# Batch 0 turned in whole blocks, output weights prepared while it is pooled, and a planner that weighs TensorE's work by array area

## The chip, the cores and the metric

One core of a Trainium2 chip runs the kernel. The metric is the device time in microseconds of one launch, from inputs in HBM to the output in HBM. The engines are TensorE (PE; its weight loads are listed as PEld), VectorE (DVE), ScalarE (ACT) and GpSimd (POOL); SyncE (SP) issues nearly all transfers. Each engine runs its instructions in the order in which the program lists them.

## The reference

Four batches of 12608 rows of 128 floats go through two attentions with 32 inducing points, and then each row goes through a feed-forward block with 1024 hidden values.

```python
def mab(q, kv):                         # per batch
    s = scale * (q @ kv.T); a = exp(s - s.max(-1)); a /= a.sum(-1) + 1e-9
    return a @ kv
h   = mab(inducing, x)                  # 32 x 128: x is pooled over all rows
y   = mab(x, h)                         # 12608 x 128
hid = y @ w_in                          # 12608 x 1024
e   = exp(hid - hid.max(-1)); solu = hid * e / (e.sum(-1) + 1e-9)
ln  = (solu - mean(solu)) / sqrt(var(solu) + 1e-6) * g_ln
out = ln @ w_out                        # 12608 x 128
```

The weights come as 64-bit floats.

## The kernel before

**Tiling.** A batch is 99 slots of 128 rows (the last is half full). Three stages work on it. `p1(b, k)` pools x in nine groups of up to 12 slots. `p2(b, j)` computes the second attention's normalised exponentials for up to 12 slots. `main()` then takes each slot as a *tile*: four matmuls give the 1024 hidden values in PSUM (L1058), VectorE scales them and takes the minimum (L1093), ScalarE exponentiates (L1103), GpSimd multiplies (L1108), ScalarE squares and sums (L1123), VectorE transposes in 32x32 blocks (L1136), and for each four tiles `products` accumulates 128 matmuls with the output weights `wc` on TensorE (L1183). There are 396 tiles. While a batch's tiles run, the next batch is pooled between them; batch 0 has nothing to hide behind.

**Pooling of batch 0.** `p1(0, k)` loads a group (L429), turns each slot on TensorE, and ScalarE copies the turned group to SBUF (L676). Turning is done by `turned_rows` (L595): four transposes of 32 rows for each slot, in two halves `w`, one for each pair of row quarters. Then come scores (L722), a running maximum through VectorE and a small matmul (L741 to L774), exponentials on ScalarE (L785), a VectorE transpose (L805), the pooling matmuls (L815) and the sum `acc` (L829, L831). The turned x goes to a DRAM buffer (L695) and is read again by `p2` (L909). Loads go to a list of buffers, EARLY_X, that borrows memory free at that time: two pieces of `wc`, seven of `spare` and two of its own. The exponentials borrow pieces of `wc` and of the output staging `os`.

**Weights.** `rounded` (L471) turns 64-bit floats to 32-bit ones in integer steps on VectorE (L483 to L492, L501), one on ScalarE (L494) and products and sums on GpSimd (L497 to L504). `weights_in` does it for w_in, `weights_out` for w_out, through the same five scratch buffers `conv`, so each step of the second waits for one of the first. `weights_out` then multiplies by the gains (L526), takes the mean over 1024 with matmuls (L535), subtracts it (L540), waits until all of batch 0 is pooled, because `wc` is lent, and spreads the rows over `wc` with 16 transfers (L556). The mean's PSUM tile comes from H, which is filled by `handover`.

**Handover.** `handover()` waits for the last pooled group, for the hidden weights of batch 0 (`hw_ready`, last copy L883) and for the first two `p2` groups' reads; then it closes the early PSUM pool and gives its banks and the borrowed SBUF to the tiles.

**The order.** Nothing is scheduled at run time. A planner runs while the program is built: each task yields operations with a cost in nanoseconds and a priority, and `Planner.run` picks for each engine, among the operations that would be ready, the one with the smallest priority. Constants at the head of the file (PR_..., P1_..., WOUT, WIN, LATE, FILL) shift these priorities. `_pe` models TensorE's clock from the busy share of stretches, and where TensorE would be idle for more than FILL ns, `_fill` puts in filler transposes of the identity (L564). The program begins with 32 such transposes (`warm`, L573).

Of the kernel before, what the change touches and what calls it, by code (L numbers as in the profile page):

```python
# [57 lines left out]
HEAD = 1  # L58
HEAD_PR = 2.3
# [9 lines left out]
P2_AHEAD = 47.6  # L69
P2_START = 24  # L70
PR_EX = -5.12
PR_EV = -13.85
PR_FI = -34.53
PR_G2 = 16.08
PR_HN = -4.97
ENDING = 16
PR_MD = 23.27
PR_MU = -7.99
PR_SQ = 2.19
PR_SA = 9.01  # L80
PR_SP = -11.4
PR_ED = -4.49
PR_EA = -8.32
PR_TU = 1.01
RUSH = 8.71
TURN_NS = 62
# [3 lines left out]
WARM = 32  # L90
WOUT = -14.2
WIN = -25.77

# [10 lines left out]
DMA_RATE = 360.0  # L104
WINDOW = 4096 / 1.2


def kind(eng):
    return "PE" if eng[:2] == "PE" else eng


class Done:


    def __init__(self, eng, end):
        self.eng, self.end = eng, end


class Op:
    def __init__(self, eng, cost, fn, *after, prio=None, alt=None, moves=0, tail=0, turn=False):  # L120
# [23 lines left out]
class Planner:  # L144


    def __init__(self, slack):
        self.clock = dict(BEGIN)
        self.ops, self.blocked, self.seq, self.slack = [], 0, 0, slack
        self.window, self.busy, self.slow, self.until = 0, {}, True, 0.0  # L150
# [61 lines left out]

    def _pe(self, start, cost):

        at = start
        while True:
            k = int(at // WINDOW)
            while self.window < k:
                busy = self.busy.get(self.window, 0.0) / WINDOW
                self.slow = busy < 0.8 if self.slow else busy < 0.7  # L220
                self.window += 1
            room = max(1.0, (k + 1) * WINDOW - at)
            rate = 2.0 if self.slow else 1.0
            took = min(room, cost * rate)
            self.busy[k] = self.busy.get(k, 0.0) + max(0.0, at + took - max(at, self.until))
            at += took
            self.until = max(self.until, at)
            cost -= took / rate
            if cost < 1.0:
                return at - start  # L230
# [38 lines left out]
    def run(self):  # L269
        clock = self.clock  # L270
        while self.ops:
# [22 lines left out]
            op.fn()  # L294
            end = start + (self._pe(start, cost) if kind(eng) == "PE" else cost)
            for e in PARTS.get(eng, (eng,)):
# [10 lines left out]
def set_attention_then_solu_kernel(ctx: ExitStack, tc: tile.TileContext, x, inducing, w_in, w_out, g_ln, out):  # L307
# [32 lines left out]
    def buf(shape, name, dtype=F32, where=None):  # L340
        return (where or const).tile(shape, dtype, name=name)
# [33 lines left out]
    S2 = Lock([(buf([P, AG, M], f"s2_{i}"), buf([P, AG], f"mx{i}"), buf([P, AG], f"nr{i}")) for i in range(2)])  # L375
    A4 = Lock([buf([P, AG * 2 * M], "a4")])
    AT = Lock([(buf([P, AG // 2, P], f"aT{i}"), buf([P, AG], f"rn{i}")) for i in range(2)])
# [90 lines left out]
    hw_ready, wc_ready, ind_ready = [Event() for _ in range(NB)], Event(), Event()  # L468
    w_in_ready = Event()

# [45 lines left out]
    def weights_out():  # L516
        wg2 = hn_b[2]
        wg = wg2.rearrange("p (k d) -> p k d", k=KC)
        g = yield from rounded(wg2, w_out.bitcast(U32).rearrange("(k p) d -> p k d", p=P), conv, conv_free, conv_end, WOUT)
        for i in range(EUS):  # L520
            give(EU, eu_b[:, i, :], g)
        give(HN, hn_b[1], g)
        gd = yield dma(4096, lambda: nc.sync.dma_start(g_sb, g_ln.rearrange("(k p) -> p k", p=P)))

        def gain(k):
            return lambda: nc.scalar.activation(wg[:, k, :], wg[:, k, :], AF.Copy, scale=g_sb[:, k : k + 1])  # L526

        for k in range(KC):
            d = yield Op("ACT", 251, gain(k), g, gd, prio=LATE)
# [7 lines left out]
        d = yield Op("PE", KC * 215, mean, g, rel, prio=LATE)  # L537
        d = yield Op(
# [3 lines left out]
            ),  # L542
            d, prio=LATE,
        )
        give(H, mp, d)
        for k in range(NP):
            yield p1_done[0][k]
        o = yield Op("POOL", 200, lambda: nc.gpsimd.memset(wc[:, :, C : C + 1], 1.0), [d for e in p1_done[0] for d in e.after])
        o_end = [o]
        rows = wc.rearrange("p (k q) d -> p k q d", q=4)  # L550
        spread = []
        for a in range(4):
            for q in range(4):
                c = yield dma(
                    M * FF * 4,
                    lambda: nc.sync.dma_start(rows[a * M : (a + 1) * M, :, q, :C], wg[q * M : (q + 1) * M]), d, o, issue=600, prio=LATE,  # L556
                )
                spread.append(c)
# [9 lines left out]
    def points():  # L568
# [5 lines left out]

        yield Op("PE", 107 * WARM, warm)
        d = yield dma(M * C * 4, lambda: nc.sync.dma_start(ind_sb, inducing))
# [61 lines left out]
    each = PG * C  # L638
    wc_flat = wc.rearrange("p j d -> p (j d)")
    EARLY_X = Lock([f[:, i * each : (i + 1) * each].rearrange("p (s c) -> p s c", c=C) for f, n in ((wc_flat, 2), (spare, SPARES * FF // each)) for i in range(n)] + xn_b)  # L640
    EARLY_T = Lock([vt_all[:, i * each : (i + 1) * each].rearrange("p (s t) -> p s t", t=P) for i in range(3 * GS * FF // each)] + [xT_b])
    e2 = [wc_flat[:, 2 * each : 2 * each + PG * M], wc_flat[:, 2 * each + PG * M : 2 * each + 2 * PG * M]] + [o.rearrange("p s c -> p (s c)")[:, : PG * M] for o in os_b[:2]]
    EARLY_EW = Lock([(e2[i], e2[i + 1].rearrange("p (s m) -> p s m", m=M)) for i in (0, 2)] + [ew_b])
# [6 lines left out]
    def p1(b, k):  # L650
# [23 lines left out]
        def copy(w, tr, d):  # L674
            def go():
                nc.scalar.copy(in_rows(xT[:, :n, :], w), from_rows(tr, n))  # L676

            d = yield Op("ACT", 94 + 48 * n, go, d, rel, tuple(ready), prio=None if early else RUSH)
# [5 lines left out]
        for w in range(2):  # L684
            tr, trel = yield ltr
            d = yield from turned_rows(tr, [(xn[:, s, :], P) for s in range(n)], w, None if early else RUSH, *[d for d, _ in xd], *trel)
            spawn(copy(w, tr, d), PRIO_P1(b, k))
        if early:
# [58 lines left out]
        if early:  # L747
# [6 lines left out]
            )  # L754
            d = yield Op("PE", 250, lambda: nc.tensor.matmul(mq, lhsT=fold2, rhs=v["mdiag"], start=True, stop=True), d, rel)
        else:
# [636 lines left out]
    for k in range(NP):  # L1393
        spawn(p1(0, k), PRIO_P1(0, k))
    spawn(weights_in(), -16)
    spawn(weights_out(), WOUT)
    spawn(handover(), 0)
# [30 lines left out]
```

## Time and profile before

| | us |
|---|---|
| median of three runs | 1169.65 |
| lowest, highest | 1164.29, 1173.36 |
| span of the profiled execution | 1170.7 |

The profile is of a further execution and gives its span, from the first to the last instruction; no separate time stands beside it. In its rows an engine's busy time is a union of its instructions; "x" counts them. [...] The ends of matmuls are modelled, so neighbouring rows of TensorE overlap by some 0.07 us. A releaser in square brackets names what ended an engine's idle time.

### The profile page before, as it was taken

To read this page: it belongs to the slowest core of one execution; us is meant where nothing else is said; L and a number is where in the kernel's file an instruction comes from. 1 tells how busy PE (TensorE), PEld (TensorE's weight loads), DVE (VectorE), ACT (ScalarE), POOL (GpSimd) and SP (SyncE) were. 2 spreads that over 40 slices of the span, in tenths; PEclk is the share of its full clock that TensorE was granted. 3 is DMA by queue.
4 is the path that set the end of the run, shared out by engine and by line. 5 is a ranking of instruction groups with operands and counts; after the bars stand their busy time and mean duration, and the time that the engine had idled before them with its cause. 6 is when DMAs were issued, how large, how long until landed. Compare 5 with 4: busy or idle time off the path is not lost.

```text
span 1170.7 us, 69841 instructions
## 1 busy us (share of the span) xinstructions
PE 1148.1 (98%) x31176; PEld 1037.0 (89%) x31176; DVE 1095.0 (94%) x1732; ACT 1105.3 (94%) x2325; POOL 1042.8 (89%) x648
## 2 busy tenths in 40 slices
PE   9989999999999999999999999999999999999997
PEld 7658988989899988999899998898899999989997
DVE  4679999999999999999999999999999999999995
ACT  4579999999999999999999999999999999999995
POOL 2379899888989999899999999899999999999994
PEclk8679999999999999999999999999999999999999
DMA  9472254453245245353223445453132323121112
GB/s 354 174 140 77 66 155 107 108 156 85 58 95 151 63 119 168 93 164 65 79 43 118 114 115 136 115 138 105 36 92 38 98 38 93 38 83 25 26 42 64
DMA packets 203405, 117.99 MB, mean 101 GB/s; under 512 B 148160, under 2 KB 156256, under 8 KB 202976
## 3 DMA queue, kind: packets, MB, share of 16 engines
q1 hardware_dynamic: 202928, 113.46, 36.5%
q8 instruction: 244, 4.00, 1.5%
q14 instruction: 57, 0.47, 0.1%
q10 hardware_dynamic: 176, 0.07, 0.0%
HBM read 53.57 MB, written 51.50 MB: 90 GB/s over the span
## 4 chain that ended last, share of the span: by engine, by line
PE 62%; ACT 11%; POOL 10%; DVE 7%; issue 5%; DMA 3%; SPq 1%; POOLq 0%; ACTq 0%; DVEq 0%
PE op L1183 43%; PE h L1058 6%; POOL eu L1108 5%; ACT sq L1123 4%; ACT eu L1103 4%; DVE vt L1136 3%; PE h L595 3%; POOL xn L1108 2%; DVE spare L1093 2%; PE h L940 2%; PE h L722 2%; DVE hn L1093 1%; PE h L815 1%; PE bank_t L595 1%; POOL xT L1108 1%
## 5 line engine op out<-in xcount | busy, mean ns | idle before, releaser
L1183 PEld LDWEIGHTS op<-wc,vt 32*128 32x128 f32 x25600 | 937.2, 185 | 52.2 <-issue 35.4
L1183 PE MATMUL op<-wc,vt 32*128 32x129 f32 x25600 | 970.2, 273 | 3.4 <-issue 1.0
L1108 POOL TENSOR_TENSOR eu<-spare,eu 128x1024 f32<-128x1024 f32 x231 | 545.7, 2382 | 27.5 <-ACT eu L1103 27.4
L1136 DVE STREAM_TRANSPOSE vt<-eu 128x1024 f32<-128x1024 f32 x351 | 429.1, 1231 | 4.7 <-POOL eu L1108 4.4
L1058 PE MATMUL h<-hs,aT 32*128 32x512 f32 x1584 | 409.0, 609 | 2.3 <-ACT xT L676 0.8
L1123 ACT ACTIVATE sq<-eu 128x1024 fp8e4<-128x1024 f32 x351 | 367.4, 1050 | 3.0 <-POOL eu L1108 3.0
L1093 DVE TENSOR_SCALAR_CACHE_REDUCE spare<-h,rn 128x1024 f32<-128x1024 f32 x247 | 309.1, 1255 | 9.9 <-PE h L1058 7.2
L1108 POOL TENSOR_TENSOR eu<-hn,eu 128x1024 f32<-128x1024 f32 x118 | 279.5, 2378 | 21.7 <-ACT eu L1103 21.3
L1103 ACT ACTIVATE eu<-spare,nm 128x1024 f32<-128x1024 f32 x232 | 265.2, 1144 | 0.9 <-DVE vt L1136 0.3
L1093 DVE TENSOR_SCALAR_CACHE_REDUCE hn<-h,rn 128x1024 f32<-128x1024 f32 x149 | 186.6, 1256 | 6.5 <-PE h L1058 4.5
L1058 PEld LDWEIGHTS h<-hs,aT 32*128 32x128 f32 x1584 | 123.1, 187 | 18.5 <-issue 6.3
L1103 ACT ACTIVATE eu<-hn,nm 128x1024 f32<-128x1024 f32 x119 | 136.1, 1144 | 1.4 <-DVE hn L1093 0.8
L1108 POOL TENSOR_TENSOR xn<-hn,xn 128x1024 f32<-128x1024 f32 x30 | 71.0, 2381 | 0.1
L1123 ACT ACTIVATION_READ_ACCUMULATOR sq<-eu 128x1 f32 x351 | 68.0, 194 | 0.0
L1282 ACT ACTIVATE os<-spare,fin 128x128 f32<-128x128 f32 (+1 forms) x200 | 62.0, 390 | 3.2 <-DMA out_dram<-os 1.8
L595 PE MATMUL h<-ident,xn 32*128 32x32 f32 x1188 | 46.4, 220 | 3.1 <-DMA xn<-in_x_dram 2.7
L595 PEld LDWEIGHTS h<-ident,xn 32*128 32x128 f32 x1188 | 45.0, 137 | 4.7 <-DMA xn<-in_x_dram 3.1
L1103 ACT ACTIVATION_READ_ACCUMULATOR eu<-spare,nm 128x1 f32 x232 | 44.9, 193 | 0.0
L676 ACT COPY xT<-h 128x768 f32<-128x768 f32 (+2 forms) x54 | 39.5, 733 | 1.8 <-PE h L1058 0.7
L1209 DVE COPY spare<-op 128x387 f32<-128x387 f32 (+1 forms) x75 | 36.0, 508 | 4.8 <-PE op L1183 4.3
L987 ACT COPY aT<-h 128x384 f32<-128x384 f32 (+3 forms) x82 | 32.7, 408 | 8.1 <-PE h L595 8.1
L595 PEld LDWEIGHTS h<-ident,a 32*128 32x128 f32 (+1 forms) x800 | 34.6, 137 | 6.3 <-issue 2.4
(187 smaller groups left out, 963.7 us busy)
## 6 DMA issues: line engine op xcount, KB each, us to landing
xT<-xd SPq DMA_DIRECT2D x93, 256.0 KB, 3.6
out_dram<-os SPq DMA_DIRECT2D x78, 256.0 KB, 3.2
xd<-xT SPq DMA_DIRECT2D x73, 256.0 KB, 3.2
xn<-in_x_dram SPq DMA_DIRECT2D x72, 256.0 KB, 3.5
dl<-dd SPq DMA_DIRECT2D x396, 1.0 KB, 2.6
a<-a SPq DMA_DIRECT2D x27, 192.0 KB, 4.3
xd<-vt SPq DMA_DIRECT2D x6, 768.0 KB, 7.2
spare<-in_x_dram SPq DMA_DIRECT2D x5, 768.0 KB, 10.9
```

The lines of the kernel that those rows point to most:

```text
L595: nc.tensor.transpose(out=tr[:h, at : at + M], in_=block[rows, :h], identity=ident[rows, rows])
L676: nc.scalar.copy(in_rows(xT[:, :n, :], w), from_rows(tr, n))
L987: lambda: nc.scalar.copy(in_rows(aT[:h, qa:qb, :], w), from_rows(tr, nq)[:h, qa:qb]),
L1058: nc.tensor.matmul(hp[:, cols], lhsT=aT[rows, i // 2, :], rhs=hs[rows, cols], start=True, stop=True)
L1093: lambda: nc.vector.tensor_scalar(out=hn, in0=hp, scalar1=rn, scalar2=None, op0=ALU.mult, op1=ALU.min, accum_out=nm),
L1103: "ACT", 1133, lambda: nc.scalar.activation(e, hn, AF.Exp, bias=nm, scale=-1.0, accum_out=G["qe"][:, s, 1:2]), d, rel, srel,
L1108: return lambda: eng.tensor_tensor(out=e, in0=hn, in1=e, op=ALU.mult)
L1123: nc.scalar.activation(sq_b[0], e, AF.Square, scale=1.0 / 32.0, saturate=False, accum_out=G["qe"][:, s, 0:1])
L1136: lambda: nc.vector.transpose(out=G["vtb"][:, : n * FF].rearrange("p (j s t) -> p j s t", j=M, s=n)[:, :, s, :], in_=e.rearrange("p (a f) ...
L1183: nc.tensor.matmul(op[a - 2 * w][:rows, i * (C + 1) : (i + 1) * (C + 1)], lhsT=vt[q, k, :], rhs=wc[q, k, :], start=(k == 0), stop=(k == JB ...
L1209: return lambda: eng(F["raw"][:rows, 2 * w + a, at : at + k, :].rearrange("p j c -> p (j c)"), op[a][:rows, : k * (C + 1)])
L1282: nc.scalar.activation(os[:rows, q, :], raw[:, q, :], AF.Copy, scale=y[:, i0 + q : i0 + q + 1])
```

## The change

- **Turning.** For batch 0, `p1` turns each slot with one transpose of the whole 128x128 block and ScalarE copies each group in two contiguous pieces of about half its slots (`blocks`, `copy_blocks`). The other batches keep `turned_rows`.
- **Buffers.** EARLY_X loses the two pieces of `wc`. The exponentials of pooling borrow the second attention's `a4` in place of `wc`; `a4` is given to that attention once all of batch 0 is pooled.
- **Output weights.** `weights_out` gets its own scratch for the raw words and two integer steps (in `wc`); two further buffers are still shared with `weights_in`. The gains are loaded first. The mean uses an early PSUM bank. The spreading no longer waits for the end of pooling, only for the subtraction and the memset of ones. `handover` also waits for the subtraction (`centred`).
- **Priorities.** w_in's read goes from -25.77 to -18.5 (x of group k has -20 + k), w_out's from -14.2 to -16.5. The tasks start at IN_PR and OUT_PR, and gain, mean, subtraction and spreading use MEAN_PR.
- **Planner.** Each TensorE operation has a share, the part of the array's activity that it counts for (0.22 for the small transposes, 0.97 for whole blocks, 0.8 and 0.48 for others); `_pe` raises the clock above WAKES and drops it below SLEEPS. Some twenty constants change, among them FILL, P1_STEP and PR_SQ.

```diff
-FILL = 296.11
+FILL = 403.68
-P1_FROM = 2.89
+P1_FROM = 4.09
-P1_STEP = 7.04
+P1_STEP = 7.35
-PR_FI = -34.53
+PR_FI = -20.13
-PR_SQ = 2.19
+PR_SQ = 16.13
-WOUT = -14.2
-WIN = -25.77
+WOUT = -16.5
+WIN = -18.5
+IN_PR = -16.22
+OUT_PR = -23.39
+MEAN_PR = -2.69
...
+WAKES, SLEEPS = 0.75, 0.43
...
+        self.share = (0.22 if turn else 0.8 if eng == "PE" else 0.48) if share is None else share
...
-                self.slow = busy < 0.8 if self.slow else busy < 0.7
+                self.slow = busy < WAKES if self.slow else busy < SLEEPS
...
-            self.busy[k] = self.busy.get(k, 0.0) + max(0.0, at + took - max(at, self.until))
+            self.busy[k] = self.busy.get(k, 0.0) + took * share
...
-        g = yield from rounded(wg2, w_out.bitcast(U32).rearrange("(k p) d -> p k d", p=P), conv, conv_free, conv_end, WOUT)
+        wide = wc.rearrange("p j d -> p (j d)")
+        own = [wide[:, : 2 * FF], wide[:, 2 * FF : 3 * FF], wide[:, 3 * FF : 4 * FF]] + conv[3:]
+        gd = yield dma(4096, lambda: nc.sync.dma_start(g_sb, g_ln.rearrange("(k p) -> p k", p=P)))
+        clear = [Event() for _ in range(3)]
+        for e in clear:
+            plan.set(e)
+        after = dict(zip(("raw", "rest", "bits"), clear), mag=conv_free["mag"], power=conv_free["power"])
+        g = yield from rounded(wg2, w_out.bitcast(U32).rearrange("(k p) d -> p k d", p=P), own, after, conv_end, WOUT)
...
-        mp, rel = yield H
+        mp, rel = yield EARLY_PB
...
-        for k in range(NP):
-            yield p1_done[0][k]
-        o = yield Op("POOL", 200, lambda: nc.gpsimd.memset(wc[:, :, C : C + 1], 1.0), [d for e in p1_done[0] for d in e.after])
+        plan.set(centred, d)
+        o = yield Op("POOL", 200, lambda: nc.gpsimd.memset(wc[:, :, C : C + 1], 1.0), g)
...
+        def copy_blocks(c0, c1, tr, d, pieces):
+            def go():
+                nc.scalar.copy(xT[:, c0:c1, :].rearrange("p s t -> p (s t)"), tr[:, : (c1 - c0) * P])
+
+            d = yield Op("ACT", 94 + 107 * (c1 - c0), go, d, rel)
...
+        def blocks(c0, c1, tr):
+            def go():
+                for s in range(c0, c1):
+                    nc.tensor.transpose(out=tr[:, (s - c0) * P : (s - c0 + 1) * P], in_=xn[:, s, :], identity=ident)
...
+        if early:
+            cuts = [0] + ([GS] if not k and n > GS else [n // 2] if n > 1 else []) + [n]
+            for c0, c1 in zip(cuts, cuts[1:]):
+                tr, trel = yield ltr
+                d = yield Op("PE", 20 + 108 * (c1 - c0), blocks(c0, c1, tr), [d for d, at in xd if at < c1], *trel, share=0.97)
+                spawn(copy_blocks(c0, c1, tr, d, len(cuts) - 1), PRIO_P1(b, k))
...
+        give(A4, a4_b, *done)
-        for e in [hw_ready[0]] + near["read"]:
+        for e in [hw_ready[0], centred] + near["read"]:
```

## Rows read from the trace of the kernel before

**Rows 1.** The page: span, and busy time of each engine (share) xinstructions.
```profile
span 1170.7 us, 69841 instructions
PE 1148.1 (98%) x31176; PEld 1037.0 (89%) x31176; DVE 1095.0 (94%) x1732; ACT 1105.3 (94%) x2325; POOL 1042.8 (89%) x648
```

**Rows 2.** Busy time in stretches; stretch, its length, then columns as headed.
```profile
core 0: us, PE busy (x) PEld busy (x) DVE busy (x) ACT busy (x) POOL busy (x), PEclk, DMA share, GB/s
8.70:22.46 13.76, 13.70 (x307) 10.57 (x307) 7.44 (x27) 8.32 (x14) 7.75 (x7) 1.00 1.05 384
23.20:47.10 23.90, 23.90 (x303) 15.96 (x298) 12.21 (x41) 11.79 (x27) 5.50 (x6) 0.50 0.67 261
47.10:53.50 6.40, 6.40 (x125) 5.26 (x122) 5.00 (x23) 1.84 (x7) 3.91 (x5) 1.00 0.72 196
74.40:84.64 10.24, 10.24 (x88) 6.99 (x88) 5.87 (x9) 6.96 (x14) 7.33 (x5) 0.50 0.90 149
...
8.70:53.50 44.80, 44.14 (x731) 31.95 (x731) 24.68 (x91) 22.65 (x48) 17.16 (x17) 0.73 0.80 291
...
100.00:1100.00 1000.00, 991.69 (x27856) 907.38 (x27854) 972.70 (x1489) 986.55 (x2064) 937.66 (x561) 1.00 0.36 93
```

**Rows 3.** Timeline, pooling at full clock: start, us, engine, line, operation, count.
```profile
5.75 0.69 DVE L483 TENSOR_SCALAR eu<-eu 128x1024 uint32<-128x1024 uint32 x1 [3.10 <-DMA eu<-in_moe_w_in_dram]
...
7.47 1.31 PE L564 MATMUL bank_e<-ident 128*128 128x128 f32 x10
8.71 1.46 PE L595 MATMUL bank_t<-ident,wc 32*128 32x32 f32 x48
19.19 0.86 PE L815 MATMUL bank_e<-wc,os 128*32 128x128 f32 x24
20.63 1.28 PE L595 MATMUL bank_t<-ident,spare 32*128 32x32 f32 x42
49.87 2.16 PE L564 MATMUL bank_t<-ident 128*128 128x128 f32 x18
53.07 0.43 PE L815 MATMUL bank_e<-spare,ew 128*32 128x128 f32 x8
```

**Rows 4.** The same timeline where the granted clock is 0.50.
```profile
24.44 2.27 PE L595 MATMUL bank_t<-ident,spare 32*128 32x32 f32 x46
26.64 1.51 PE L815 MATMUL bank_e<-spare,ew 128*32 128x128 f32 x24
44.06 1.54 PE L564 MATMUL bank_e<-ident 128*128 128x128 f32 x6
```

**Rows 5.** Groups by line, 2 to 3 us, then 6.6 to 7.4 us: busy, mean ns.
```profile
L573 PE MATMUL bank_t<-ident 128*128 128x128 f32 x7 | 1.7, 417 | 0.0
...
L573 PE MATMUL bank_t<-ident 128*128 128x128 f32 x8 | 1.0, 272 | 0.0
```

**Rows 6.** Busy time of line 564 alone, PE and PEld, in two stretches.
```profile
8.70:47.10 38.40, 5.18 (x26) 3.42 (x25) 0.69 0.82 307
...
100.00:1170.00 1070.00, 0.88 (x6) 0.64 (x6) 1.00 0.35 91
```

**Rows 7.** Timeline of SP, ScalarE, TensorE and VectorE around the output weights.
```profile
14.54 0.37 SPq L478 DMA_DIRECT2D eu<-in_moe_w_out_dram  x1
...
58.41 0.58 ACT L883 COPY hs<-bank_e 128x512 f32<-128x512 f32 x1 [0.17 <-PE bank_e L880]
...
60.07 2.05 PE L535 MATMUL h<-hn,ones_mean 128*128 128x128 f32 x16
...
62.16 1.22 DVE L540 TENSOR_TENSOR hn<-h,hn 128x1024 f32<-128x1024 f32 x1
```

**Rows 8.** Timeline of SP, VectorE and TensorE as the tiles begin.
```profile
70.12 6.84 SPq L556 DMA_DIRECT2D wc<-hn  x10
...
80.47 0.58 DVE L948 STREAM_TRANSPOSE s<-h 128x384 f32<-128x384 f32 x1 [3.58 <-PE h L940]
...
81.82 0.58 PE L1183 MATMUL op<-wc,vt 32*128 32x129 f32 x2
```

More of the change, by code (lines that the diff above doesn't have):

```diff
@@ L58 @@
 HEAD = 1
-HEAD_PR = 2.3
+HEAD_PR = 2.06
 RETIRE = 5
@@ L77 @@
 PR_MD = 23.27
-PR_MU = -7.99
-PR_SQ = 2.19
-PR_SA = 9.01
+PR_MU = -4.03
+PR_SQ = 16.13
+PR_SA = 8.04
 PR_SP = -11.4
 PR_ED = -4.49
-PR_EA = -8.32
-PR_TU = 1.01
-RUSH = 8.71
+PR_EA = -7.87
+PR_TU = -0.44
+RUSH = 6.77
 TURN_NS = 62
@@ L119, with __init__ @@
 class Op:
-    def __init__(self, eng, cost, fn, *after, prio=None, alt=None, moves=0, tail=0, turn=False):
+    def __init__(self, eng, cost, fn, *after, prio=None, alt=None, moves=0, tail=0, turn=False, share=None):
         self.eng, self.cost, self.fn, self.after, self.prio, self.alt, self.moves, self.tail, self.turn = eng, cost, fn, after, prio, alt, moves, tail, turn
+        self.share = (0.22 if turn else 0.8 if eng == "PE" else 0.48) if share is None else share
 class Event:
@@ L149, in __init__ @@
         self.ops, self.blocked, self.seq, self.slack = [], 0, 0, slack
-        self.window, self.busy, self.slow, self.until = 0, {}, True, 0.0
+        self.window, self.busy, self.slow = 0, {}, True
         self.fill, self.scratch, self.data, self.now = None, (), 0.0, 0.0
@@ L211, in free, with _pe @@
         return max(self.clock[e] for e in PARTS.get(eng, (eng,)))
-    def _pe(self, start, cost):
+    def _pe(self, start, cost, share=1.0):
         at = start
@@ L294, in run @@
             op.fn()
-            end = start + (self._pe(start, cost) if kind(eng) == "PE" else cost)
+            end = start + (self._pe(start, cost, op.share) if kind(eng) == "PE" else cost)
             for e in PARTS.get(eng, (eng,)):
@@ L528, in weights_out @@
         for k in range(KC):
-            d = yield Op("ACT", 251, gain(k), g, gd, prio=LATE)
+            d = yield Op("ACT", 251, gain(k), g, gd, prio=MEAN_PR)
         g = [d]
-        mp, rel = yield H
+        mp, rel = yield EARLY_PB
         def mean():
@@ L535, in mean @@
                 nc.tensor.matmul(mp[:, :C], lhsT=ones_mean, rhs=wg[:, k, :], start=(k == 0), stop=(k == KC - 1))
-        d = yield Op("PE", KC * 215, mean, g, rel, prio=LATE)
+        d = yield Op("PE", KC * 215, mean, g, rel, prio=MEAN_PR, share=1.0)
         d = yield Op(
@@ L555, in weights_out @@
                     M * FF * 4,
-                    lambda: nc.sync.dma_start(rows[a * M : (a + 1) * M, :, q, :C], wg[q * M : (q + 1) * M]), d, o, issue=600, prio=LATE,
+                    lambda: nc.sync.dma_start(rows[a * M : (a + 1) * M, :, q, :C], wg[q * M : (q + 1) * M]), d, o, issue=600, prio=MEAN_PR,
                 )
@@ L573, in warm @@
                 nc.tensor.transpose(out=tr_b[:, :P], in_=ident, identity=ident)
-        yield Op("PE", 107 * WARM, warm)
+        yield Op("PE", 107 * WARM, warm, share=1.0)
         d = yield dma(M * C * 4, lambda: nc.sync.dma_start(ind_sb, inducing))
@@ L638, in set_attention_then_solu_kernel @@
     each = PG * C
[L639 to L640 removed]
+    EARLY_X = Lock([f[:, i * each : (i + 1) * each].rearrange("p (s c) -> p s c", c=C) for f, n in ((spare, SPARES * FF // each),) for i in range(n)] + xn_b)
     EARLY_T = Lock([vt_all[:, i * each : (i + 1) * each].rearrange("p (s t) -> p s t", t=P) for i in range(3 * GS * FF // each)] + [xT_b])
[L642 removed]
+    e2 = [a4_b[:, i * PG * M : (i + 1) * PG * M] for i in range(2)] + [o.rearrange("p s c -> p (s c)")[:, : PG * M] for o in os_b[:2]]
     EARLY_EW = Lock([(e2[i], e2[i + 1].rearrange("p (s m) -> p s m", m=M)) for i in (0, 2)] + [ew_b])
@@ L676, in go @@
                 nc.scalar.copy(in_rows(xT[:, :n, :], w), from_rows(tr, n))
-            d = yield Op("ACT", 94 + 48 * n, go, d, rel, tuple(ready), prio=None if early else RUSH)
+            d = yield Op("ACT", 94 + 48 * n, go, d, rel, tuple(ready), prio=RUSH)
             give(ltr, tr, d)
@@ L682, in copy @@
                 plan.set(copied, *ready)
[L684 to L687, printed above, removed]
+        def copy_blocks(c0, c1, tr, d, pieces):
+            def go():
+                nc.scalar.copy(xT[:, c0:c1, :].rearrange("p s t -> p (s t)"), tr[:, : (c1 - c0) * P])
+            d = yield Op("ACT", 94 + 107 * (c1 - c0), go, d, rel)
+            give(ltr, tr, d)
+            ready.append(d)
+            if len(ready) == pieces:
+                plan.set(copied, *ready)
+        def blocks(c0, c1, tr):
+            def go():
+                for s in range(c0, c1):
+                    nc.tensor.transpose(out=tr[:, (s - c0) * P : (s - c0 + 1) * P], in_=xn[:, s, :], identity=ident)
+            return go
+        if early:
[4 more added lines that the diff above has]
+                spawn(copy_blocks(c0, c1, tr, d, len(cuts) - 1), PRIO_P1(b, k))
+        else:
+            for w in range(2):
+                tr, trel = yield ltr
+                d = yield from turned_rows(tr, [(xn[:, s, :], P) for s in range(n)], w, RUSH, *[d for d, _ in xd], *trel)
+                spawn(copy(w, tr, d), PRIO_P1(b, k))
         if early:
@@ L754, in p1 @@
             )
-            d = yield Op("PE", 250, lambda: nc.tensor.matmul(mq, lhsT=fold2, rhs=v["mdiag"], start=True, stop=True), d, rel)
+            d = yield Op("PE", 250, lambda: nc.tensor.matmul(mq, lhsT=fold2, rhs=v["mdiag"], start=True, stop=True), d, rel, share=0.02)
         else:
@@ L1394, in set_attention_then_solu_kernel @@
         spawn(p1(0, k), PRIO_P1(0, k))
[L1395 to L1396 removed]
+    spawn(weights_in(), IN_PR)
+    spawn(weights_out(), OUT_PR)
     spawn(handover(), 0)
```

17 lines of the change are left out of this document (8 added, 9 removed).

## The prediction

> **What bounds the kernel now.** I read the page first. Four engines are busy for 89 to 98% of the span [rows 1], so the average names no bound and the stages have to be taken apart. The windows view does that [rows 2]. From 100 to 1100 us, ScalarE is the engine with least slack but for TensorE, whose busy time overlaps itself: 986.55 of 1000 us. Its idle time is 13.4 us, some 37 ns for each of the roughly 365 tiles in them (396 over some 1085 us). VectorE stands behind it with 972.70 us. Nothing in the change takes work off ScalarE there, so this stretch should keep its length, and what can move is when it starts.
>
> The stretch before it has another limit. Batch 0 is pooled from 8.71 us [rows 3] to 53.5 us. [...] The timeline of TensorE shows what the lower level costs: 24 pooling matmuls take 0.86 us at full clock and 1.51 us at half; the 32x32 transposes go from 1.28 us for 42 to 2.27 us for 46 [rows 3, 4].
>
> **The transposes.** Each 128-row slot is turned by four 32x32 transposes now, and by one whole one after. At full clock the small ones cost 1.28/42 x 4 = 122 ns a slot and 18 whole ones 2.16/18 = 120 ns [rows 3], so 99 slots save 0.2 us: the instruction count is not the gain. At half clock it is 2.27/46 x 4 = 197 ns against 1.54/6 = 257 ns [rows 4]: there the whole block is dearer by 60 ns. ScalarE's copies move the same elements in two pieces a group; I cost them at nothing, hidden by ScalarE's idle half of the stretch; without that cover an extra 0.1 us a group would be 0.9 us.
>
> The question is whether the clock stays up. It fell at 23.2 us after a stretch of small transposes, pooling and score matmuls. The nearest rows on whole blocks are the 32 warm-up transposes, before which TensorE has done nothing else: between 2 and 3 us they take 417 ns each, from 6.6 us on 272 ns [rows 5]. (The windows view prints a clock of 1.00 for these first microseconds; I go by the durations.) So whole blocks alone have brought the clock up. The small ones did not keep it up at 23 us, and it came back only near 47 us, after a stretch with six whole ones in it [rows 2, 4].
>
> [...]
>
> **What the pooling is worth.** With TensorE at full clock and setting the pace, 23.90 us would become 11.95. But then VectorE would need 12.21 us in 11.95, so it becomes the limit. I size the phase by VectorE. It is busy for 24.68 us between 8.70 and 53.50 us [rows 2]. The read of the input weights moves behind x of groups 0 and 1 in SP's queue, so their first rounding steps, which now run from 5.75 us on [rows 3], fall into the phase: 8.7 - 5.75 = 2.9 us. That gives 27.6 us. At what density can it run? At full clock it was 7.44/13.76 = 54% while the pipeline filled, and 5.00/6.40 = 78% from 47.10 to 53.50 us [rows 2]. I take 78%, as the pipeline is full most of the time: 27.6/0.78 = 35.4 us. The phase can begin once the warm-up is over: 10 filler blocks stand between its end and the first turn, 1.2 us before 8.71 [rows 3], because x waited behind the weights' megabyte; x now goes first. So it runs from 7.5 to 42.9 us instead of to 53.5: **10.6 us**. Bounds: at 54% it ends at 58.6, no gain and 5.1 us lost, if VectorE's waits were as long as in the filling; with TensorE halved and VectorE in its shadow, 11.95 + 1.2 = 13.2 us. TensorE's 26 fillers, 5.18 us of that phase [rows 6], are room for the mean that moves in (2.05 us).
>
> The wc tensor is no longer lent as two x buffers: 11 become 9, for 9 groups, so no load waits. The exponentials move to the attention's a4, which is first wanted after pooling. One 4 KB load of the gains is moved ahead in SP's queue: at most 0.5 us, hidden by the warm-up.
>
> **The output weights.** Now they are rounded late: their read is issued at 14.54 us, the mean runs at 60.07 to 62.12 on TensorE and the subtraction from 62.16 on VectorE, directly ahead of the first softmax row of a tile [rows 7]. Moved into the pooling, the subtraction's 1.22 us leave that path: **1.2 us**. The mean's 2.05 us lie beside the first tiles' own preparation; bounds 0 and 1.2 + 2.0 = 3.2. As handover now waits for the subtraction, everything behind it would stand if it came late (second rival).
>
> The 16 spreading transfers (the last ten hold SP's queue for 6.84 us, up to 77 us [rows 8]) move to the time after the subtraction. There, each one can hold a reload or a store of x behind it for about 0.7 us; stores come first needed a group of 12 tiles later, so I cost this at nothing, and at 0.7 us a reload if two meet. The first product now starts at 81.82 us [rows 8], behind those transfers. And VectorE idles 3.58 us ahead of 80.47 us for score matmuls at half clock [rows 8], in a stretch (74.40 to 84.64) with ScalarE busy for 6.96 of 10.24 us [rows 2]. Products that can start as soon as four tiles are turned keep TensorE busier here. I take half of the 3.6 us, as matmuls at full clock take about half: **1.8 us**, bounds 0 and 3.6.
>
> **The planner.** The constants and the area-weighted clock model cost nothing themselves; they reorder all engines. Fillers play no part later: six from 100 us on [rows 6]. For the reordering of the steady stretch I take 0, within what a ScalarE idle of 13.4 us [rows 2] allows: gaining half of it or losing as much is 7 us either way, and 4 us I hold for likely.
>
> **The sum.** 10.6 + 1.2 + 1.8 = 13.6 us. The profiled execution's span is 1170.7 us, 1.05 us above the median of the three timed runs (1169.65), so I make no correction: 1170.7 - 13.6 = **1157.1 us**, 1157.
>
> **The rivals.**
> *The clock falls all the same.* The scores and pooling matmuls between the blocks use 32 columns of the array at a time, and when small transposes joined them the clock fell. For it: VectorE's and ScalarE's waits leave TensorE gaps. Against: the warm-up rows. Half of the slots would be turned at the lower level, 50 x 60 ns = 3 us dearer, and 1.2 (start) + 1.2 (subtraction) are kept: about 1171 us. [...]
> *Handover waits for the output weights.* From the read's issue to the subtraction's end now takes 63.4 - 14.5 = 48.8 us [rows 7]. The read would go at about 4 us (an estimate: it stands behind some seven issues in place of 14); at the same length it ends at 52.8, where the hidden rows are due at 59.0 - 10.6 = 48.4 (their last copy ends at 59.0 [rows 7]). It costs 4.4 us: 1161.5. Against: much of the 48.8 us was a low priority, with VectorE idle.
> *Slower: late squares.* ScalarE's square of a tile gets a priority of 16.13 tiles behind instead of 2.19, while each of the five buffers of exponentials is held until its square is done. If they run out, the next exponential waits for a product and a square. Each 37 ns a tile over some 390 tiles is 14.4 us, the whole gain; that is as much again as ScalarE's idle now. Beyond 70 ns it is slower by over 1%; at 100 ns, 1157 + 39 = 1196 us. For it: ScalarE is the fullest engine [rows 2]. Against: when no exponential can start, the squares are what ScalarE has left to run, so buffers come free.
> *A better steady order*: 7 us of ScalarE's idle go too: 1150 us.
>
> **How the numbers follow.** The forecast has 0.60 and its own range is 1150 to 1163; the clock falls 0.11; handover waits 0.13; slower 0.07; better order 0.09. About 1% (11.7 us, so 1158.0) is what a measurement of this kernel can tell from no change. Two thirds of the forecast's chance lie below that, 0.40, with the better order 0.49: faster 0.49. Slower 0.07. The rest, 0.20 + 0.11 + 0.13, is 0.44. The range leaves out the slower case and the fallen clock, and reaches from 1149 to 1168.
>
> **What would show it.** The granted clock from 20 to 45 us: 1.00 if the main step is right, 0.50 for the first rival. VectorE's last pooling sum ends near 43 us. The subtraction (one 1.2 us instruction of VectorE) lies before the last copy of the hidden rows; if that copy is done and TensorE then idles, it is the second rival. The first product starts some 15 us before 81.8. ScalarE's busy time from 100 to 1100 us stays near 987; less, with exponentials waiting for squares, is the third. The forecast is wrong if pooling ends early and the span doesn't follow: then the steady stretch gave it back.

## The result and the profile after

The changed kernel takes 1173.07 us (median of 12 runs, 1167.36 to 1178.89) against 1167.03 for the kernel before (12 runs beside it): the ratio is 1.0051, 95% interval 1.0027 to 1.0076. It is slower by 0.5%, or about 6 us, where 1157 was forecast: outside the range.

The page of the changed kernel, to be held against [rows 1]:

```profile
span 1171.8 us, 69231 instructions
...
PE 1142.6 (98%) x30887; PEld 1031.6 (88%) x30887; DVE 1094.9 (93%) x1732; ACT 1105.1 (94%) x2320; POOL 1044.9 (89%) x647
```

The engines do the same work: ScalarE is busy for 1105.1 us against 1105.3. What differs is where it idles. In stretches (columns as in [rows 2]; PEclk is the granted clock of TensorE as a share of the full one):

```profile
24.10:27.50 3.40, 3.40 (x35) 2.83 (x27) 2.03 (x8) 1.45 (x4) 2.13 (x3) 0.50 1.06 410
61.70:82.20 20.50, 20.06 (x146) 12.99 (x147) 15.18 (x24) 15.19 (x31) 16.61 (x9) 0.50 0.54 112
...
100.00:1100.00 1000.00, 987.58 (x27766) 902.19 (x27763) 967.22 (x1481) 982.86 (x2054) 935.28 (x561) 1.00 0.36 93
```

While batch 0 is pooled TensorE is at half clock for 3.40 us in place of 23.90, in all of which it was busy, VectorE and ScalarE in about half [rows 2]. But it is at half clock from 61.7 to 82.2 us, as the tiles begin, and from 100 to 1100 us ScalarE idles for 17.1 us in place of 13.4. The timelines of VectorE and ScalarE show the head:

```profile
47.72 0.35 DVE L863 SCALAR_TENSOR_TENSOR acc<-acc,small,bank_e 128x128 f32<-128x128 f32 x1
49.67 1.23 DVE L550 TENSOR_TENSOR hn<-bank_e,hn 128x1024 f32<-128x1024 f32 x1 [1.60 <-PE bank_e L545]
...
54.29 0.59 ACT L915 COPY hs<-bank_e 128x512 f32<-128x512 f32 x1 [0.17 <-PE bank_e L912]
...
57.94 1.28 DVE L1125 TENSOR_SCALAR_CACHE_REDUCE hn<-h,rn 128x1024 f32<-128x1024 f32 x1 [0.19 <-PE h L1090]
```

In the trace of before the same two instructions, the last pooling sum and the first of a tile, are

```profile
53.56 0.35 DVE L831 SCALAR_TENSOR_TENSOR acc<-acc,small,bank_e 128x128 f32<-128x128 f32 x1
...
63.30 1.27 DVE L1093 TENSOR_SCALAR_CACHE_REDUCE hn<-h,rn 128x1024 f32<-128x1024 f32 x1
```

The last pooling sum ends at 48.1 us (53.9 before, 42.9 forecast), the output weights' subtraction stands ahead of the hidden rows, and the first tile starts at 57.94 us in place of 63.30. So a lead of 5.4 us is there, and the span doesn't have it.

A ledger of ScalarE's idle time says when it went. Both kernels do the same ScalarE work (some 1107 us in this count, which joins its instructions' intervals), so spans differ by idle time. Worked out from the two traces, in us:

| | before tile 1 | tiles 1 to 30 | 31 to 130 | 131 to 230 | 231 to 330 | to 395 | tail |
|---|---|---|---|---|---|---|---|
| before | 34.0 | 6.1 | 3.0 | 5.6 | 3.6 | 1.1 | 9.7 |
| after | 29.0 | 9.0 | 7.6 | 4.4 | 3.1 | 1.8 | 9.8 |

The head gains 5.0, and 6.6 are given back behind it: 2.9 in the first 30 tiles and 4.6 in the next hundred, of which later tiles win back a little.

### The profile page after: what moved, and what is told of

Same layout as the page of the kernel before. It is cut to its first block, busy times and chain, and to the rows that moved or that the text cites. A ratio compares the mean times of both kernels' runs of the same rounds, so it can differ in the third digit from the quotient of the medians.

```text
span 1171.8 us, 69231 instructions
## 1 busy us (share of the span) xinstructions
PE 1142.6 (98%) x30887; PEld 1031.6 (88%) x30887; DVE 1094.9 (93%) x1732; ACT 1105.1 (94%) x2320; POOL 1044.9 (89%) x647
## 4 chain that ended last, share of the span: by engine, by line
PE 45%; POOL 21%; ACT 11%; DVE 8%; issue 6%; DMA 5%; SPq 3%; POOLq 0%; ACTq 0%; DVEq 0%
PE op L1215 32%; POOL eu L1140 12%; PE h L1090 5%; ACT eu L1135 4%; POOL xn L1140 4%; ACT sq L1155 3%; DVE vt L1168 3%; DVE spare L1125 2%; PE h L604 2%; POOL xT L1140 2%; DVE hn L1125 1%; DMA wc<-in_moe_w_out_dram 1%; PE h L847 1%; PE h L754 1%; DMA a<-a 1%
## 5 line engine op out<-in xcount | busy, mean ns | idle before, releaser
L1215 PEld LDWEIGHTS op<-wc,vt 32*128 32x128 f32 x25600 | 934.3, 185 | 52.1 <-issue 35.1
L1140 POOL TENSOR_TENSOR eu<-spare,eu 128x1024 f32<-128x1024 f32 x203 | 478.5, 2381 | 35.0 <-ACT eu L1135 32.4
L1140 POOL TENSOR_TENSOR eu<-hn,eu 128x1024 f32<-128x1024 f32 x149 | 351.2, 2377 | 18.9 <-ACT eu L1135 18.5
L1125 DVE TENSOR_SCALAR_CACHE_REDUCE spare<-h,rn 128x1024 f32<-128x1024 f32 x247 | 308.9, 1256 | 11.4 <-PE h L1090 9.7
L1135 ACT ACTIVATE eu<-spare,nm 128x1024 f32<-128x1024 f32 x203 | 231.7, 1143 | 0.3
L1135 ACT ACTIVATE eu<-hn,nm 128x1024 f32<-128x1024 f32 x149 | 170.2, 1144 | 3.5 <-DVE hn L1125 3.5
L1090 PEld LDWEIGHTS h<-hs,aT 32*128 32x128 f32 x1584 | 124.4, 187 | 23.2 <-issue 9.7
L1140 POOL TENSOR_TENSOR xn<-spare,xn 128x1024 f32<-128x1024 f32 x29 | 69.4, 2417 | 0.0
L604 PE MATMUL h<-ident,a 32*128 32x32 f32 (+1 forms) x800 | 36.4, 218 | 6.1 <-DMA a<-a 4.0
L1241 DVE COPY spare<-op 128x387 f32<-128x387 f32 (+1 forms) x72 | 33.6, 496 | 8.3 <-PE op L1215 8.1
## 6 DMA issues: line engine op xcount, KB each, us to landing
spare<-in_x_dram SPq DMA_DIRECT2D x5, 768.0 KB, 10.6
```

The source lines that it names most:

```text
L604: nc.tensor.transpose(out=tr[:h, at : at + M], in_=block[rows, :h], identity=ident[rows, rows])
L1090: nc.tensor.matmul(hp[:, cols], lhsT=aT[rows, i // 2, :], rhs=hs[rows, cols], start=True, stop=True)
L1125: lambda: nc.vector.tensor_scalar(out=hn, in0=hp, scalar1=rn, scalar2=None, op0=ALU.mult, op1=ALU.min, accum_out=nm),
L1135: "ACT", 1133, lambda: nc.scalar.activation(e, hn, AF.Exp, bias=nm, scale=-1.0, accum_out=G["qe"][:, s, 1:2]), d, rel, srel,
L1140: return lambda: eng.tensor_tensor(out=e, in0=hn, in1=e, op=ALU.mult)
L1215: nc.tensor.matmul(op[a - 2 * w][:rows, i * (C + 1) : (i + 1) * (C + 1)], lhsT=vt[q, k, :], rhs=wc[q, k, :], start=(k == 0), stop=(k == JB ...
```

## The experiments

Two questions: is it the planner's new order of the long stretch (theory "order"), or the new start (theory "head")? And what takes the lead away at the first tiles? Each kernel's time is set against runs of before beside it on the same chip, and these ratios are what I compare; the runs below fall into four sets of four, each on a chip of its own.

**How much an order is worth by chance.** One planner cost, that of a TensorE step (BEAT, 223.4 ns), is changed by 0.2%; hardly an instruction changes, only their order.

```diff
-BEAT = 223.4
+BEAT = 223.0
```

> The changed kernel with one planner cost, BEAT, at 223.0 ns instead of 223.4. The early part keeps its order; from some 80 us on the order of all engines differs. Theory N (the loss lies in the luck of the greedy order once tiles run): the median moves by several us against the changed kernel's 1173, to anywhere between 1163 and 1178, while the first tile still starts near 57.9 us. Theory C (the retuned constants cost it): it stays at 1171 to 1175, as the constants are the same. Theory K (the low clock from 61 to 82 us costs it): 1171 to 1175 too.

> The kernel before with BEAT at 223.0 instead of 223.4: the same early order, another order of the tiles' work later. Theory N: several us away from 1167, either way. Theories C and K: within 2 us of the kernel before.

Measured: the changed kernel goes to 1169.16 us, ratio to before 1.0004 (0.9981 to 1.0027), and the kernel before to 1185.07, ratio 1.0137 (1.0094 to 1.0180). Both fit the first theory, that a free order is a matter of luck. Then the fourteen ordering constants that both kernels share and the change resets (FILL, P1_STEP, PR_SQ and the like) are exchanged:

> The changed kernel with the fourteen planner constants that both kernels have (FILL, HEAD_PR, P1_FROM, P1_STEP, P2_AHEAD, PR_..., RUSH) set back to those of the kernel before; whole blocks, the early output weights and the new clock model stay. Theory C: the early lead of about 2.4 us at 90 us is kept to the end, 1162 to 1166. Theory N: anywhere in 1160 to 1178. Theory K: 1171 to 1175.

> The kernel before with the same fourteen constants set to those of the changed kernel; nothing else. Theory C: 1172 to 1178, the steady stretch loses some 8 us. Theory N: anywhere in 1160 to 1178. Theory K: within 2 us of the kernel before.

Measured: 1186.83 us, ratio 1.0155 (1.0117 to 1.0192), and 1182.37 us, ratio 1.0108 (1.0067 to 1.0148). Both times lie above every range put down for them. Either kernel is slower with the other's constants, by 12 to 13 us, and one cost moved by 0.2% is worth from -5 to +16 us. Whether each set of constants fits its own kernel, or any new order would have cost as much, these runs don't tell. A difference of 6 us between two free orders says nothing of the change's parts unless the order is held.

**The order held.** The order that the planner chose for before was recorded, and from the first tile on the planner takes its next operation from that record; the steps of the output weights stay free.

```diff
+            pick = self._scripted(pick)
             self.ops = [o for o in self.ops if o[3] != pick[3]]
```

> A control for the next three: the kernel before, whose planner is made to repeat its own recorded order from the first tile's matmuls on (the output weights' steps alone stay free). Each engine's list is that of the kernel before up to which of two equal buffers is named. Every theory: within 2 us of the kernel before, 1165 to 1171.

> The whole early part of the changed kernel (whole blocks, early output weights, new clock model), with the fourteen shared constants and, from the first tile's matmuls on, the recorded order of the kernel before. Theory S (the early part is worth some 2 to 5 us in the mean of many executions, and the loss was the new order of the tiles' work): 1163 to 1167, faster than the control by 2 to 5 us; first tile near 56.5 us; mean granted clock 0.988 against 0.984. Theory Z (the early part is worth nothing or less once its own order is taken out): the control's time or above. My forecast of 13.6 us would be 1155.

> The kernel before with whole 128x128 blocks for batch 0 alone, order of the tiles' work held to that of the kernel before. Theory S: the granted clock stays at 1.00 in pooling and the mean clock rises to 0.986 or more; 1164 to 1168. Theory Z: the control's time.

> The kernel before with the output weights rounded, centred and spread during pooling (own scratch, early PSUM bank, new read priorities), small transposes kept, order of the tiles' work held to that of the kernel before. Theory S: the clock falls in pooling as before, and what VectorE and GpSimd do twice at a time there costs about what the subtraction saves: within 2 us of the control. Theory Z: above the control by 2 us or more.

Measured: 1170.87 us for the control, ratio 1.0049 (1.0023 to 1.0075); 1203.54 and 1198.50 us for the two with blocks (1.0328 and 1.0302); 1171.42 us for the early weights alone (1.0040, 1.0016 to 1.0063), no different from the control. The control should have been 1.000: with the same sequence on VectorE, ScalarE and GpSimd it is 0.5% slower (at a mean granted clock of 0.989, against 0.986 for before beside it), and what makes it so (other buffers behind the same names, free spreads) stays open. Differences below 0.5% between held and free kernels are therefore not read as effects.

The two with blocks had not been held: ScalarE's copies of xT in the later batches had changed places with one another, since the record named them by a count that the new early copies shift. It costs nothing until a batch's end, and there it costs a lot. The waits of the run with blocks alone, 330 to 440 us (us in total, times, longest):

```profile
DVE spare L1595 <- PE h L1560: 9.0, 6, 2.4
...
ACT a L1465 <- POOL s L1458: 5.5, 1, 5.5
POOL s L1458 <- DVE mx L1455: 5.3, 1, 5.3
```

One chain of softmax weights arrives late and all engines stand in line behind it; between tiles 100 and 130 that run loses 16 us to its control. With the copies named by batch the order is the same on every engine. Heads are planned freely, with the constants of the kernel whose order is held:

> The changed kernel's head (whole blocks, early output weights) with the work from the first tile on in the order of the kernel before, on every engine. In the earlier run of this kind (1203.5 us) the xT copies of batches 1 to 3 had been given one another's places; here each keeps its own. Theory 'order' (the steady order is what the change lost, the new head is worth 2 to 5 us): 1166 to 1169 us, below the held control's 1170.9. Rival 'head' (the head's lead is lost again to the half clock around the first tiles, or the blocks disturb the steady part): 1171 to 1176 us.

> The kernel before with whole blocks in batch 0 alone, its order from the first tile on held on every engine, the xT copies of the later batches too (in the run at 1198.5 us these had changed places). Theory 'order': the loss of that run was the shuffled copies, so 1167 to 1171 us, at or below the held control's 1170.9. Rival 'blocks disturb the steady part': 1180 us or more once again.

> The kernel before's head (small turns, output weights later) with the work from the first tile on in the order of the changed kernel, on every engine. Theory 'order': it has the changed kernel's slower order and not its head, so the changed kernel's 1173 us plus 2 to 5 us: 1175 to 1178 us. Rival 'head': the changed kernel is slow through its head, so without it 1165 to 1170 us.

Measured: the changed head in before's order 1165.77 us, ratio 0.9985 (0.9961 to 1.0008); blocks alone 1165.93 us, 1.0006 (0.9985 to 1.0026); before's head in the changed order 1173.62 us, 1.0070 (1.0045 to 1.0095). Each is 0.2 to 1.4 us under the range of theory "order". By order and head, as ratios to before:

| head | before's order | changed order |
|---|---|---|
| old | 1 (free), 1.0049 (held) | 1.0070 (held) |
| changed | 0.9985 (held) | 1.0051 (free) |

So "blocks disturb the steady part" falls. For the changed head "order" is borne out: the changed order costs 1.0051/0.9985 = 1.0066, 7.7 us, some 4 us either way. For the old head it isn't shown: against its held control the changed order costs 0.2%, inside both intervals. The changed order with the old head is as slow as the changed kernel, within the intervals, and with the new head in before's order the loss is gone. The head itself is worth 1.7 us against before, which its interval doesn't tell from nothing, and 7.5 against the held control, which ran on another chip; those are the bounds.

**The clock at the first tiles.** The fillers there turn 96x96 pieces; in this run they use the whole array.

```diff
-        nc.tensor.transpose(out=bank[:, :n], in_=ident[:n], identity=ident[:n, :n])
+        if n == P:
+            nc.tensor.transpose(out=bank[:, :n], in_=ident[:n], identity=ident[:n, :n])
+        else:
+            nc.tensor.matmul(bank[:, :n], lhsT=ident, rhs=ident[:, :n], start=True, stop=True)
```

> The changed kernel, its plan untouched, but a filler that has 96 columns free is a matmul over all 128 rows and 128 columns of the array instead of a 96x96 turn. Theory 'clock at the first tiles': the clock is back before 82 us (the half clock of 61.7 to 82.2 us is cut short), and the time falls by 2 to 5 us to 1168 to 1171 us. Rival 'the handover stalls on the buffers, not on the clock': the clock may come back, but the time stays at 1172 to 1174 us; longer fillers in front of real work could make it 1175 us.

Measured: 1172.74 us, ratio 1.0055 (1.0031 to 1.0078), and the granted clock is 0.50 from 60.1 to 80.5 us all the same. The experiment didn't change what it was to change, so of the price of that clock it says nothing. Two held runs bear on its effect at the eighth tile. The control had full clock from 63.4 us on, the changed head in the same order had half from 61.3 to 81.8 us, and the eighth tile started at 76.9 and 76.8 us: something else sets it. Nor can the clock as a whole be the loss: the mean granted clock of the changed kernel's 12 runs is 0.989, that of 30 runs of before 0.985. It has a price all the same. Over those 30 runs, one with a mean lower by 0.01, which is some 23 us at half clock, took 8.6 us longer (a correlation of -0.8; it doesn't say in which stretch).

**SyncE's queue.** With blocks alone the first tile starts at 49.13 us, 14.2 earlier than before, and the eighth only 4.6 earlier; against its held control it is 7.1 and 0.5. The timelines of SyncE, TensorE and VectorE in that run:

```profile
55.09 11.39 SPq L1034 DMA_DIRECT2D wc<-hn  x16
66.53 0.60 SPq L1411 DMA_DIRECT2D xT<-xd  x1
67.25 0.70 SPq L1469 DMA_DIRECT2D a<-a  x1
...
72.02 0.53 PE L1073 MATMUL h<-ident,a 32*128 32x32 f32 x6 [2.91 <-DMA a<-a]
...
75.91 0.58 DVE L1450 STREAM_TRANSPOSE s<-h 128x384 f32<-128x384 f32 x1 [10.99 <-PE h L1442]
76.42 1.24 DVE L1595 TENSOR_SCALAR_CACHE_REDUCE hn<-h,rn 128x1024 f32<-128x1024 f32 x1
```

The 16 spreads take 11.39 us to issue, 0.71 us each, and behind them stands a<-a, the transfer that doubles the softmax weights of the next tiles; TensorE turns these only when it has landed, and VectorE, which needs TensorE's matmuls behind that, stands for 10.99 us. Four runs move only the spreads, behind that a<-a, with the order held (in the last one the changed kernel's own order):

```diff
         spread = []
+        yield a_gone
...
             dp = yield dma(P * n * M * 8, lambda: nc.sync.dma_start(a2[:, :n, 1, :], a2[:, :n, 0, :]), de)
+            if a_gone.after is None:
+                plan.set(a_gone)
```

> As the run of whole blocks alone with the order held exactly (1165.9 us; first tile at 49.1, eighth at 76.4 us), but the 16 DMAs that spread the output weights stand behind the transfer a<-a of the second set of softmax weights on SyncE's queue instead of ahead of it (there they took 55.1 to 66.5 us and a<-a left at 67.25). Nothing else moves. Theory 'queue' (the lead at the first tile dies because a<-a stands behind 11.4 us of spreads): a<-a leaves at 54 to 58 us, the eighth tile comes at 64 to 69 us instead of 76.4, and the time falls by 4 to 8 us to 1158 to 1162 us. Rival 'elsewhere' (another wait of the second group is as late, or the first products now wait for the spreads): the eighth tile stays later than 73 us and the time at 1164 to 1168 us.

> The changed kernel's head with the order of before held exactly (1165.8 us; a<-a left at 64.5 us, eighth tile at 76.8 us), the 16 spreads behind a<-a on SyncE's queue. Theory 'queue': a<-a some 4 us earlier or more, the eighth tile at 68 to 73 us, the time 1160 to 1163 us. Rival 'elsewhere': the eighth tile still at 75 us or later, 1164 to 1168 us.

> The kernel before with its own order held (1170.9 us for that control; first tile at 56.2, eighth at 76.9 us, a<-a at 69.2 behind spreads from 56.5 to 67.9), the 16 spreads behind a<-a. Theory 'queue': a<-a leaves at 60 to 63 us, the eighth tile at 69 to 72 us, the time 1164 to 1167 us. Rival 'elsewhere': 1168 to 1173 us.

> The changed kernel with its own order held exactly (that order, not before's), the 16 spreads behind a<-a on SyncE's queue (in the changed kernel a<-a left at 63.6 us amid the spreads). Theory 'queue' and 'order' together: a gain of 2 to 4 us at the eighth to tenth tile that this slower order may swallow, 1168 to 1172 us. If the changed order were not slower in itself, 1162 to 1166 us like the run of the changed head in before's order.

Starts in the table are us in one trace each.

| kernel | ratio to before | a<-a issued | tile 1 | tile 8 | tile 9 | tile 16 |
|---|---|---|---|---|---|---|
| before (free order) | 1 | 69.4 | 63.3 | 81.0 | 85.0 | 101.5 |
| blocks, held | 1.0006 | 67.3 | 49.1 | 76.4 | 80.5 | 98.3 |
| blocks, held, spreads behind | 0.9953 (0.9933 to 0.9972) | 55.8 | 49.3 | 66.3 | 73.3 | 90.4 |
| all, held | 0.9985 | 64.5 | 56.6 | 76.8 | 80.9 | 97.4 |
| all, held, spreads behind | 0.9993 (0.9972 to 1.0013) | 61.0 | 56.6 | 70.5 | 79.0 | 96.9 |
| before, held | 1.0049 | 69.2 | 56.2 | 76.9 | 79.7 | 96.7 |
| before, held, spreads behind | 1.0012 (0.9984 to 1.0040) | 62.7 | 58.2 | 72.2 | 78.7 | 95.2 |
| changed kernel | 1.0051 | 63.6 | 57.9 | 73.0 | 78.9 | 98.3 |
| the same, spreads behind | 1.0044 (1.0025 to 1.0063) | 61.4 | 56.7 | 71.0 | 80.9 | 99.3 |

With blocks alone the theory "queue" holds as foretold up to the eighth tile: a<-a leaves 11.5 us earlier, the eighth tile comes 10.1 us earlier, eight of them are still there at the sixteenth, and the time is 1162.71 us, just above the 1158 to 1162 expected. That version is faster than before by 0.5%, and than the changed kernel (1.0051) by 1%. Its rows:

```profile
55.80 0.70 SPq L1471 DMA_DIRECT2D a<-a  x1
56.59 11.86 SPq L1036 DMA_DIRECT2D wc<-hn  x16
...
71.33 0.51 PE L1689 MATMUL op<-wc,vt 32*128 32x129 f32 x8 [0.25 <-DMA wc<-hn]
...
73.31 1.28 DVE L1599 TENSOR_SCALAR_CACHE_REDUCE hn<-h,rn 128x1024 f32<-128x1024 f32 x1 [4.10 <-PE h L1564]
```

Where a<-a itself comes later, the spreads behind it come too late. With the whole changed head a<-a left only 3.5 us earlier, at 61.0. The eighth tile did come 6.3 us earlier, but the time stayed at 1168.51 us, against 1160 to 1163 expected, and the ninth tile shows why:

```profile
61.78 11.27 SPq L1045 DMA_DIRECT2D wc<-hn  x16
...
75.63 0.51 PE L1697 MATMUL op<-wc,vt 32*128 32x129 f32 x8 [1.07 <-DMA wc<-hn]
...
79.01 1.28 DVE L1607 TENSOR_SCALAR_CACHE_REDUCE hn<-h,rn 128x1024 f32<-128x1024 f32 x1 [5.65 <-PE h L1572]
```

The first products now stand on TensorE waiting for the last spreads, and the next tiles' hidden matmuls stand behind them in its order. Ahead of a<-a or behind it, the same 11.3 us of issuing are in the way: "elsewhere" was right for this head. The old head (1170.45 us, where 1164 to 1167 was expected) gains 0.37% on its control, within both intervals: unclear. The changed kernel with its own order stays at 1174.79 us, ratio 1.0044, where 1168 to 1172 was expected: its loss isn't in this queue.

These four runs also hold the cleanest pairs, on one chip and with the spreads alike. *Order:* the changed head takes 1174.79 us in its own order and 1168.51 in before's, both held; the means are 5.7 us apart, 2 either way. ScalarE idles 11.5 us in tiles 1 to 30 and 6.1 in 31 to 130 with the one, 8.4 and 2.9 with the other: the losses of the ledger above come back with the order alone. *Output weights:* with blocks and without the rest of the changed head it is 1162.71 us, with the whole changed head 1168.51; the means are 5.9 us apart, 2 either way. That rest is the early output weights and the planner's new model of TensorE's clock.

## Why the prediction was wrong

Two steps of the sum failed. It carried 10.6 + 1.2 us of an earlier first tile to the end of the kernel, where the whole changed head brings next to none against most traces of the old one. And it put the new order of the steady stretch at 0, where that order costs some 6 us and makes the kernel slower.

**Whole blocks hold the clock: right in ten of eleven traces.** In the three traces with blocks alone the granted clock is 1.00 from the warm-up to 60 us or later, here in the run with order held:

```profile
24.00:48.00 24.00, 22.54 (x285) 14.81 (x287) 17.14 (x64) 15.26 (x42) 9.80 (x12) 1.00 0.81 312
```

In seven of the eight with the whole changed head it is so too; in the changed kernel's own it fell for 3.4 us. In the six with the old head it falls while batch 0 is pooled, for 3.4 to 23.9 us. Over all the timed runs the mean granted clock was 0.994 with blocks (12 runs, order held) and 0.985 for before (30 beside them). In the run with blocks alone TensorE does nothing but 96x96 turns from 59.15 to 69.1 us (row in the last section), at a granted clock of 1.00. The first rival (1171) is near the measured time by luck: the clock that it needs didn't fall.

**The 10.6 us for the pooling: taken from one unlucky execution.** The old head started its first tile at 63.3, 55.3, 57.9, 56.2, 56.2 and 58.2 us in six traces, of six builds. The first two have the same order up to there and differ by their time at half clock in pooling, 23.9 and 3.4 us. The one before me when I worked it out was the latest of them, with the longest time at half clock. The base was high too: in the runs of the result a time is some 2 us above the span of the same run, so the profiled span of 1170.7 belongs to a time near 1172.5, 5.5 above the median of 1167.03. Seen from the middle of the six (57 us) blocks alone bring the first tile to 49.2, which is 8 us; the whole changed head, at 55.8 to 57.9 us in its eight traces, brings next to nothing.

**The output weights, +1.2: wrong sign.** Moved early, they cost the first tile what the blocks gain: 49.2 us without, 56.6 with, and with the spreads moved out of the way 5.9 us of the time. Most of it is lost in the pooling: the last sum ends at 40.7 us with blocks alone and at 46.5 with the whole changed head (both with before's order held, both at full clock until then). The rest is lost behind it. The mean and the subtraction stand between the last sum and the hidden rows (49.67 in the rows above): from the last sum to the last copy of the hidden rows it is 6.8 us, where before it was 5.1 (53.9 to 59.0). It is not the second rival, which put 4.4 us on a handover that waits: the subtraction ends at 50.9 us, ahead of that copy. Of the 5.8 us in the pooling a part is that the rounding got dearer there, which I had priced at its old durations; for w_out VectorE's steps take 1.4 us more in all. The rest wasn't taken apart. The rows of the changed kernel:

```profile
20.70 0.76 DVE L488 TENSOR_SCALAR wc<-wc 128x1024 uint32<-128x1024 uint32 x1 [1.24 <-DMA wc<-in_moe_w_out_dram]
21.39 1.75 DVE L490 TENSOR_SCALAR wc<-wc 128x1024 uint32<-128x1024 uint32 x1
...
19.64 2.95 POOL L502 TENSOR_TENSOR w_in_sb<-w_in_sb,eu 128x512 f32<-128x512 f32 x2 [4.04 <-ACT w_in_sb L499]
22.55 2.94 POOL L504 TENSOR_TENSOR w_in_sb<-w_in_sb,eu 128x512 f32<-128x512 f32 x2
```

The second VectorE row takes 1.75 us for a step of the form that took 0.69 in [rows 3], while GpSimd multiplies for w_in beside it; GpSimd's pairs take 2.95 and 2.94 where the same two took 2.49 and 2.50 in the trace of before. So VectorE's step is 1.06 us longer and each pair some 0.45. The first VectorE row, beside the same work of GpSimd, is only 0.07 us longer. No run here shows the reason.

**The spreads, costed at nothing, and the lead, carried to the end: wrong.** I looked at the reloads that a single transfer could hold up, 0.7 us each, and not at all 16 together ahead of one transfer that the second set of tiles needs. With blocks alone they are 11.4 us in front of it; moved away, the time falls by 0.5% (0.9953 against 1.0006). In the changed kernel moving them gains nothing that can be told from noise (1.0044 against 1.0051), so they show why a lead shrinks, and not where its 6 us went. I also carried a lead at the first tile to the end of the kernel. The lead of blocks alone, 14.2 us at the first tile, was 4.6 at the eighth and 3.2 at the sixteenth, and against the held control 7.1, 0.5 and -1.6.

**The hiccup, 1.8 us: not seen.** In the changed kernel the first product starts at 76.76 us in place of 81.82 [rows 8], 5 us earlier where some 15 were forecast, but the clock is at half there (0.50 from 61.7 to 82.2 us); the ledger shows 2.9 us more idle time in the first 30 tiles, not less.

**The steady order, 0 within 4: mis-sized.** It costs 7.7 us, with about 4 either way, or 5.7 with 2 either way in the cleaner pair. ScalarE's waits from 85 to 424 us in the changed kernel have no one cause; where before had 0.3 us of waiting for aT's turns and 1.2 for GpSimd, it has

```profile
ACT aT L1019 <- PE h L604: 2.3, 3, 1.4
ACT sq L1155 <- POOL eu L1140: 2.3, 4, 1.2
ACT xT L684 <- PE h L1090: 1.0, 2, 0.5
ACT aT L1019 <- PE h L1090: 0.9, 1, 0.9
```

Which constant does it wasn't taken apart, and since one cost moved by 0.2% shifts the time by as much, it may be none in particular. The parts add up: 1.7 us from the head at before's order, 5.7 lost by the order, 6 measured (with 7.7 they must, as both come from the same three times). The late squares were not tried alone; ScalarE's waits in that stretch hold no exponential, which that rival needs. What the 20 us at half clock at the first tiles cost stays open.

## What to carry to other kernels

When a kernel's order comes from a planner, a change of one part is measured only with the order of the rest held, and a held order has to be checked instruction by instruction on every engine. Before a lead at the start is carried to the end, follow the next group of work through each in-order queue, that of the transfers too: many small issues in a row are one long instruction for whatever stands behind them (here 16 spreads, 11.39 us, ahead of a<-a). A clock that falls in one profile is priced from several (here for 3.4 to 23.9 us of the pooling in six traces of the old head).

## What the hardware showed that was not expected

The clock that one program is granted changes from execution to execution: over 35 runs of the kernel before its mean over a run lay between 0.978 and 0.990. With the old head TensorE was at half clock during pooling from 18.1 to 21.5, 24.3 to 34.6, 15.7 to 22.5, 24.9 to 35.1 and 23.2 to 47.1 us in five of the six traces. Its fall and return are not settled by the shape of the fillers: it stood at 1.00 through 118 turns of 96x96 from 59 to 69 us in the run with blocks alone (the drop came at 71.4, while TensorE idled for 2.9 us), while in the changed kernel it was at 0.50 with fillers of either shape. The turns of the run with blocks alone:

```profile
59.15 9.96 PE L1042 MATMUL op<-ident 96*128 96x96 f32 x118 [1.72 <-DVE spare L1595]
```
